# Windowed attention, low-rank mixing and a two-layer MLP in one kernel: the second MLP product's sums built up in one PSUM half, one form of V fewer, a new written-out order

## The chip, the cores and the metric

One Trainium2 chip, one of its cores. A kernel here is a program for five engines that run side by side and meet by semaphores: TensorE (PE; its weight loads are shown as PEld), VectorE (DVE), ScalarE (ACT), GpSimd (POOL) and SyncE (SP), plus the DMA engines that move data between device memory and the on-chip memory SBUF. TensorE writes its results into PSUM, 8 banks of 512 fp32 columns for each of 128 partitions; the other engines fetch them from there. The metric is device time of one execution in microseconds (us), lower is better. A run gives the median of several executions; a profiled execution gives the trace that the sections below read.

## The reference

Four sequences of 768 tokens, 8 heads of 64. Attention with a window of 96 keys and 8 global keys and a linear distance bias, then a mixing of tokens through a matrix of rank 32, then an MLP with a residual:

```python
scores = q @ k.T / sqrt(64) - slope[h] * dist          # dist = 96 for global keys outside the window
a = softmax(where(is_global | is_local, scores, -1e9))
x = (a @ v) as (4, 768, 512)
u = x + ((x.transpose(0, 2, 1) @ U) @ V).transpose(0, 2, 1)    # U 768x32, V 32x768
out = u + relu(u @ w_ch1) @ w_ch2                              # 512 -> 2048 -> 512
```

Inputs and output are fp32; the kernel's products take fp16 and collect in fp32.

## The kernel before

The work is cut into small tasks, each a handful of instructions on one engine, with a name, an estimated duration and the tasks that it needs. The names are used all through this document:

- **Loads.** `lk3`, `lq3`, `lv3`: keys, queries and values of pair 3 (a pair is two heads of one batch; pairs 0 to 3 are batch 0, and so on to 15). `w1_0` to `w1_3`, `w2_0` to `w2_3`: quarters of the MLP weights. All are issued by POOL, but k and q of pair 0 (`lk0`, `lq0`) and U and V (`mixl`) by SP. `Ck0`, `Cq0` cast pair 0 to fp16.
- **Attention of a pair p.** `TKp`, `TQp` transpose on PE, `EKp`, `EQp` copy the result out of PSUM. `KOp` makes a second copy of the keys whose first 32 columns of each block are the global keys; it runs on the engine that the string `KO` names for the pair (A, D, P, or S: a DMA on SP's queue). `VCp`, `VGp` do the same for V. `SBp.s` puts the bias into PSUM (batch 0 only), `Sp.s` adds the scores, `EXp.s` takes exp on ACT, `MKp.s` multiplies by a mask (batches 1 to 3), `PVp` is the product with V, `RCp` and `NMp` normalise into `x_sb`, `XCp` casts to fp16. Pair 3 does this in three parts (`PV3.s`, `RC3.s`, `NH3.s`, `UP3.s`).
- **Mixing.** `UPp` transposes x and multiplies by U, `XEp`, `XUp` turn the result, `TEp` copies it out as `tmp`, `HMp` multiplies by V, `E0p` (for the last pair of a batch `E0p`, `E1p`) copies u, transposed, to `uT`.
- **MLP-1 of batch b**: 16 units n of 128 columns; `M1ab.n` (three of the four inner parts; `M1a`, `M1c`, `M1d` one each for the first units of batch 0) and `M1bb.n` (the fourth), then `RLb.n`, the ReLU on ACT.
- **MLP-2 of batch b**: a 2x2 block product with seven block products instead of eight (Strassen's way, in Winograd's form). `PAb.g`, `PBb.g` form the sums of the ReLU's blocks on DVE, `TWag`, `TWbg` those of w2, once. For each of three tiles t of 128 rows, `RSb.t` puts the low-rank rest (V's forms times `tmp`) into PSUM, and `P1b.t` to `P7b.t` add the seven products, 8 matmuls each. The tasks `DIb.t` to `DHb.t` (D and a letter) then add what lies in PSUM into `x_sb`, and `Ob.t`, `Ob.t+3` store a finished row block through SP.

Two PSUM banks hold a tile's sums: `gX` and `gY`, each of two halves of 256 columns. Before, P1 goes to gX half 0, P6 to gX half 1, P7 to gY half 0, P5 to gY half 1; after they have been fetched P2 goes on in gX half 0, P4 in gY half 0, P3 in gY half 1. The partial sum that four output blocks share is kept in SBUF (`u2`, then `u3`): ACT copies P1 there (`DI`), DVE adds P6 (`DA`) and P7 (`DB`), and the blocks get them from there (`DD`, and `DE`, which adds u2 to two blocks at once).

What sets the order: `ORDER` is a list of all task names written out by hand (or by a search). A planner in the kernel walks through it, gives every task the earliest start that its estimates allow, chooses buffers and PSUM banks, and emits the tasks sorted by these starts. So each engine runs its own tasks strictly in one sequence, and an instruction that waits holds up all behind it on its engine. POOL's queue takes copies and DMA issues in one sequence too. Until MLP-1 of batch 0, the kernel fills gaps that the planner sees on PE with products of zeros (`idle`, L1081).

Of the kernel before, what the change touches and what calls it, by code (L numbers as in the profile page):

```python
# [21 lines left out]
wz iota vz relf rel3 bias6 ones3 bias1 bias4 bias0 lk0 Ck0 TK0 bias3 lq0 Cq0 bias5 SB0.2 TQ0 EQ0 lk1 SB0.0 ones1  # L22
ones0 TK1 EK1 KO1 bias7 lq1 TQ1 EK0 KO0 S0.2 S0.0 SB0.1 S0.1 back bias2 lq3 EQ1 ones2 lk3 TK3 EK3 EX0.0 lk2 lv0
EX0.1 lq2 lv1 lv3 lv2 EX0.2 SB1.2 TK2 S1.2 EX1.2 SB1.0 S1.0 lk4 EX1.0 lq4 SB1.1 mixl lk5 EK2 S1.1 EX1.1 VC0 VG0 TQ3
EQ3 KO2 TQ2 EQ2 PV0 RC0 SB2.2 S2.2 VC3 EX2.2 SB2.1 SB2.0 S2.0 S2.1 EX2.0 VC1 VG1 PV1 KO3 EX2.1 NM0 VG3 RC1 NM1 SB3.2
S3.2 SB3.0 S3.0 SB3.1 S3.1 XC1 EX3.2 EX3.0 VC2 VG2 u16 PV2 UP1 EX3.1 w1_0 vs2 TE1 RC2 NM2 PV3.0 TK4 EK4 vs0 HM1
mask1 E01 PV3.1 RC3.1 NH3.1 XC0 UP0 TQ4 XC2 w1_1 RC3.0 TE0 NH3.0 KO4 UP2 EQ4 HM0 E00 PV3.2 TE2 S4.2 EX4.2 HM2 E02
RC3.2 UP3.0 lq5 UP3.1 NH3.2 UP3.2 NM3 TE3 TD0 S4.0 HM3 E13 E03 M1a0.3 lv4 M1c0.3 w1_2 w1_3 EX4.1 M1d0.3 M1b0.3 RL0.3
M1a0.2 mask3 M1c0.2 w2_2 mask0 TK5 EK5 KO5 w2_0 w2_1 MK4.1 M1d0.2 M1b0.2 w2_3 RL0.2 M1a0.0 M1c0.0 EX4.0 M1d0.0 TQ5
EQ5 M1b0.0 RL0.0 M1a0.7 M1b0.7 S5.0 mask2 M1a0.6 EX5.0 RL0.7 M1b0.6 RL0.6 lk6 MK4.0 EX5.1 VC4 VG4 MK4.2 PV4 M1a0.11  # L30
M1b0.11 M1a0.8 vs3 vs1 RC4 NM4 XC4 RL0.11 lv5 M1b0.8 RL0.8 lk7 PA0.1 PB0.1 S5.2 EX5.2 MK5.0 M1a0.13 M1b0.13 MK5.2
RL0.13 M1a0.10 TWa0 M1b0.10 mask6 lq6 RL0.10 UP4 XE4 TWb0 M1a0.9 M1b0.9 RL0.9 M1a0.14 M1b0.14 RL0.14 lv7 M1a0.15
M1b0.15 MK5.1 M1a0.1 M1c0.1 RL0.15 M1d0.1 XU4 TE4 PA0.3 M1b0.1 RL0.1 M1a0.5 M1b0.5 RL0.5 M1a0.4 M1b0.4 RL0.4 TWa1
TWb1 M1a0.12 M1b0.12 PA0.0 RL0.12 TK6 EK6 PA0.2 RS0.1 P10.1 lv6 DI0.1 HM4 E04 PB0.3 RS0.0 P10.0 VC5 VG5 KO6 PV5 RC5
NM5 TK7 lq7 EK7 TQ6 P50.1 P60.1 EQ6 PB0.0 S6.2 PB0.2 mask7 P20.1 DF0.1 P60.0 mask5 EX6.2 S6.0 P70.1 DI0.0 DA0.0
DE0.0 mask4 EX6.1 MK6.2 P70.0 TQ7 KO7 P20.0 lq8 MK6.1 lk8 P50.0 lq9 EX6.0 DF0.0 DA0.1 MK6.0 DC0.0 VC6 DB0.0 DB0.1
DD0.0 EQ7 XC5 S7.0 lv8 EX7.0 RS0.2 P60.2 MK7.0 VG6 EX7.1 MK7.1 S7.2 EX7.2 P50.2 UP5 XE5 lk9 P10.2 XU5 MK7.2 DC0.2
DE0.1 P40.0 lq10 DC0.1 TE5 HM5 PV6 DI0.2 P20.2 E05 TQ10 EQ10 RC6 NM6 lk10 DA0.2 DE0.2 TK8 VC7 EK8 DG0.0 P30.1 VG7
PV7 TQ8 EQ8 RC7 TK9 NM7 P70.2 TK10 EK10 XC7 XC6 UP6 EK9 P30.2 DH0.1 TQ9 lv9 XE6 XU6 TE6 DH0.2 DB0.2 P30.0 EQ9 HM6
E06 lk11 lq14 UP7 XE7 P40.1 XU7 DD0.2 TE7 P40.2 HM7 DH0.0 KO8 VC8 VG8 S8.2 DF0.2 O0.2 E17 DG0.1 E07 EX8.2 DG0.2  # L40
M1a1.6 M1b1.6 RL1.6 KO9 S9.2 EX9.2 M1a1.9 M1b1.9 O0.1 M1a1.8 RL1.9 M1b1.8 S8.0 EX8.0 MK8.0 lq11 RL1.8 M1a1.13
M1b1.13 RL1.13 TK11 EK11 EX8.1 VC9 TQ11 M1a1.5 M1b1.5 KO11 RL1.5 M1a1.12 M1b1.12 KO10 S10.2 RL1.12 EQ11 S11.2 DD0.1
TD1 O0.5 M1a1.3 M1b1.3 M1a1.0 lk13 O0.3 O0.0 O0.4 MK8.1 EX10.2 RL1.3 MK8.2 PV8 lk12 M1b1.0 RC8 EX11.2 NM8 PA1.2
PB1.2 M1a1.4 RL1.0 M1b1.4 RL1.4 S9.0 EX9.0 MK9.0 EX9.1 MK9.1 M1a1.7 M1b1.7 M1a1.1 RL1.7 MK11.2 M1b1.1 lq12 TQ12
RL1.1 XC8 lq13 UP8 EQ12 M1a1.2 M1b1.2 VG9 M1a1.10 RL1.2 MK9.2 PV9 XE8 PA1.0 PB1.0 RC9 XU8 M1b1.10 lv14 RL1.10
# [12 lines left out]
RL2.7 M1a2.6 M1b2.6 HM14 TE12 PA2.2 PB2.2 HM12 RS2.2 RL2.6 E014 P12.2 PA2.1 PB2.1 E012 PB2.3 RS2.1 S13.0 P12.1 VC15
lv13 DI2.2 DI2.1 VC13 P22.2 DF2.2 P52.1 DC2.1 P22.1 P62.1 DA2.1 DF2.1 EX13.0 P62.2 DA2.2 P72.1 MK13.0 DE2.1 DB2.1
EX13.1 RS2.0 S15.0 EX15.0 EX15.1 P52.2 P12.0 DI2.0 MK13.1 DC2.2 VG15 MK15.1 VG13 PV13 RC13 P42.1 MK15.0 DE2.2 NM13  # L60
P62.0 PV15 RC15 DG2.1 NM15 P72.0 XC13 XC15 P52.0 P32.2 UP13 P32.1 DA2.0 DE2.0 DB2.0 P72.2 UP15 P22.0 DC2.0 DD2.0
XE13 DB2.2 XU13 XE15 XU15 DH2.1 DH2.2 O2.2 TE15 P42.0 HM15 E015 DF2.0 TE13 HM13 P42.2 DG2.2 E013 P32.0 DH2.0 DG2.0
O2.0 E115 M1a3.8 M1b3.8 TD3 M1a3.10 O2.1 RL3.8 M1b3.10 M1a3.7 RL3.10 M1b3.7 M1a3.5 RL3.7 M1b3.5 M1a3.15 RL3.5
M1b3.15 M1a3.2 RL3.15 M1b3.2 M1a3.0 RL3.2 M1b3.0 M1a3.3 RL3.0 M1b3.3 DD2.2 M1a3.1 DD2.1 O2.4 M1b3.1 RL3.3 M1a3.6
RL3.1 M1b3.6 M1a3.12 RL3.6 M1b3.12 RL3.12 M1a3.14 M1b3.14 RL3.14 M1a3.11 M1b3.11 PA3.1 M1a3.9 RL3.11 M1b3.9 M1a3.4
RL3.9 M1b3.4 M1a3.13 M1b3.13 RL3.4 RL3.13 RS3.0 O2.3 RS3.1 PB3.1 PA3.3 PB3.3 RS3.2 P13.0 P13.1 P13.2 DI3.2 PA3.0
PA3.2 P63.1 P53.0 PB3.0 P63.0 PB3.2 P73.0 P73.1 DI3.0 DA3.0 DE3.0 DB3.0 DC3.0 DD3.0 P53.1 P63.2 DA3.2 DE3.2 DI3.1
DA3.1 O2.5 P33.0 DB3.1 P23.2 DF3.2 O3.2a P73.2 DB3.2 P43.1 P43.2 DC3.1 DE3.1 DD3.1 DH3.0 P23.0 DF3.0 O3.0 DG3.1 O3.4
P53.2 DC3.2 DD3.2 DG3.2 O3.5 P23.1 DF3.1 P43.0 DG3.0 P33.1 O3.3 P33.2 DH3.1 O3.1 DH3.2 O3.2
""".split()  # L70
CFG = {
    "NU": (4, 5, 6, 7, 8, 9, 10, 11, 12, 13, 14, 15), "back": "KO1", "early": 4, "Z": (), "ZS": "DDDDDDDD", "ZR": "DDDDDDDD", "ZQ": "DDDDDDDD", "TE": "AADDAADADAAAAAAA", "XE": "DDDDDAADAAAAAAAA", "EK": "ADDDDDAAADADAAAD", "EQ": "DADAADAAAAADAAAA", "KO": "ADDDPPASPPSDAADD",
    "HR": "RRFRRFFRRRFRRRRR", "RR": "RRRRRRRRRRRR", "IB": "ADADDDDA", "U16": "D", "VS": "PPDD", "C0": "DD",
    "VO": "DDPPDPPPPPPPSSPP", "XC": "PDPDDAPDPPPPPPAA", "E": "AAAAAAAADDAAAADA",
}


class Task:
    def __init__(self, name, eng, dur, fn, deps=(), lat=0.1, acq=(), rel=(), size=0.0, parts=1, mode=0, bw=(), br=()):
        self.name, self.eng, self.dur, self.fn = name, eng, dur, fn  # L80
        self.deps = [d for d in deps if d is not None]
        self.lat = lat
        self.acq, self.rel, self.size, self.parts, self.mode = acq, rel, size, parts, mode
        self.start = self.end = None

        self.bw, self.br = bw, tuple(br) + tuple(g for g in rel if g.kind == "ps" and eng != PE)
# [11 lines left out]
class Planner:  # L98
# [41 lines left out]
    def run(self, names):  # L140
# [5 lines left out]
        dma_free = {POOL: 4.1, SP: 0.0}  # L146
        for t in (self.names[n] for n in names):
# [16 lines left out]
            for g in t.acq:  # L164
                if g.since is None:
                    g.since = s
            t.start, t.end = s, s + t.dur
            clock[t.eng] = t.end
# [30 lines left out]
def kernel(  # L199
# [52 lines left out]
    vs = sb("vs", [P, 4, HS], FP16)  # L252
# [3 lines left out]
    N_STG, N_V, N_QK, N_EP, N_X16, N_U = 3, 4, 3, 6, 3, 2  # L256
# [18 lines left out]
    td = sb("td", [P, hd], FP16, 2)  # L275
    sA = sb("sA", [P, 3, hj, HS], FP16)
    tB = sb("tB", [P, 3, hj, hd], FP16)
    u2 = sb("u2", [P, hd], FP32, N_U)
    u3 = sb("u3", [P, hd], FP32, N_U)

    assert hj == H and HS == 384
# [189 lines left out]
    def attention(p):  # L471
# [126 lines left out]
        for pt in parts:  # L598
# [9 lines left out]
            for s in pt:  # L608
                SCs[s] = SC
# [521 lines left out]
```

## Time and profile before

| | |
|---|---|
| median of 3 runs | 229.91 us (229.59, 229.91, 231.64) |
| the profiled execution: its own time | 231.71 us |
| the profiled execution: span from first to last instruction | 229.9 us, granted clock 1.00 |
| start of MLP-1 of batch 0 on PE | 29.40 us |
| MLP-2 of batch 3, first to last product | 208.29 to 226.8 us |
| MLP-1: 512 matmuls of 384 columns | L836 |
| MLP-2: 672 matmuls of 256 columns | L1011 |
| low-rank rest in MLP-2: 48 matmuls | L1001 |

The part of the profile that gives busy time counts an engine as busy while an instruction is in it. For PE the ends of matmuls are modelled, and since they overlap, a busy PE can still have small holes; the distance from one matmul's start to the next one's shows them. The trace has each DMA's issue and its landing; "waits" name what ended an engine's idle time.

### The profile page before, as it was taken

Reading aid. Unit: us, or ns where it says so; the run is one execution under the profiler, and the core shown is the slowest. Engines: PE = TensorE matmul, PEld = TensorE weight load, DVE = VectorE, ACT = ScalarE, POOL = GpSimd, SP = SyncE. Lnnn points to the kernel's source line nnn. Section 1 sums busy time; section 2 is a strip of 40 time slices with the busy share of each in tenths; the row PEclk is TensorE's granted clock in tenths of the full one; section 3 lists DMA queues with packets and bytes.
Section 4 is the critical chain, followed back from the end, with each engine's and each line's share of the span. In section 5 each row is a group of like instructions: output and inputs, shape, how many; then the busy total and the mean of one; then the engine's idle time right before and its main releaser. Section 6 shows DMA issues by size and latency. Waiting matters only on the chain.

```text
span 229.9 us, 5824 instructions
## 1 busy us (share of the span) xinstructions
PE 222.9 (97%) x2455; PEld 161.7 (70%) x2455; DVE 151.8 (66%) x314; ACT 137.4 (60%) x202; POOL 97.4 (42%) x129
## 2 busy tenths in 40 slices
PE   7799989999999999999999999999999999999994
PEld 2466846666888976666798876666689965658883
DVE  7478846789899872499566785445968650067583
ACT  3598887867785568885666448867633246562100
POOL 7879889229994997074932160400001000000000
PEclk9999999999999999999999999999999999999999
DMA  7999899999998999949596173510000043000015
GB/s 171 166 166 118 125 159 206 208 181 137 133 121 55 64 75 230 178 29 105 37 76 63 56 128 138 37 37 0 3 0 3 0 159 119 0 3 0 0 55 222
DMA packets 77193, 21.63 MB, mean 94 GB/s; under 512 B 67280, under 2 KB 74192, under 8 KB 77168
## 3 DMA queue, kind: packets, MB, share of 16 engines
q0 software_dynamic: 68320, 13.24, 68.9%
q1 hardware_dynamic: 8848, 8.03, 10.8%
q8 instruction: 19, 0.31, 0.5%
q14 instruction: 6, 0.05, 0.1%
HBM read 27.46 MB, written 6.29 MB: 147 GB/s over the span
## 4 chain that ended last, share of the span: by engine, by line
PE 89%; DMA 6%; POOL 2%; DVE 1%; issue 0%; POOLq 0%; DVEq 0%
PE ps L836 35%; PE ps L1011 32%; DMA stgq<-in_q_dram 6%; PE ps L591 5%; PE ps L504 3%; PE ps L686 3%; PE ps L659 2%; PE ps L685 2%; PE ps L572 2%; PE ps L780 1%; PE ps L1001 1%; DVE x_sb L1024 1%; PE ps L485 1%; PE ps L664 1%; POOL kO L303 0%; POOL x L748 0%
## 5 line engine op out<-in xcount | busy, mean ns | idle before, releaser
L836 PE MATMUL ps<-uT,w 128*128 128x384 f16 x512 | 87.5, 326 | 0.1
L836 PEld LDWEIGHTS <-w 128*128 128x128 f16 x512 | 48.4, 98 | 31.1 <-issue 0.2
L852 ACT ACTIVATE htr<-ps 128x768 f16<-128x768 f32 x64 | 51.7, 811 | 25.1 <-PE ps L836 24.7
L618 ACT ACTIVATE ep<-ps 128x1024 f16<-128x1024 f32 (+1 forms) x48 | 43.9, 951 | 11.3 <-PE ps L591 10.9
L1011 PEld LDWEIGHTS <-htr 128*128 128x128 f16 x384 | 35.7, 98 | 5.8 <-issue 1.4
L748 POOL CAST x<-x_sb 128x768 f16<-128x768 f32 x9 | 8.2, 910 | 63.7 <-DVE x_sb L724 55.6
L1011 PEld LDWEIGHTS <-sA 128*128 128x128 f16 x288 | 27.3, 98 | 3.7 <-issue 0.4
L1011 PE MATMUL ps<-w,sA 128*128 128x256 f16 x192 | 24.6, 273 | 0.0
L1011 PE MATMUL ps<-w,htr 128*128 128x256 f16 x192 | 24.5, 273 | 0.0
L1011 PE MATMUL ps<-tB,htr 128*128 128x256 f16 x192 | 24.0, 273 | 0.0
L1024 DVE TENSOR_TENSOR x_sb<-ps,x_sb 128x256 f32<-128x256 f32 x48 | 19.4, 417 | 4.8 <-PE ps L1011 4.2
L966 DVE TENSOR_TENSOR sA<-htr 128x768 f16<-128x768 f16 x16 | 9.2, 576 | 19.6 <-ACT htr L852 19.4
L382 POOL DMA_DIRECT2D stgk<-in_k_dram x24 | 20.1, 858 | 4.4 <-DMA w<-in_moe_w_ch_dram 2.8
L382 POOL DMA_DIRECT2D stgq<-in_q_dram x24 | 20.0, 852 | 3.5 <-DMA w<-in_moe_w_ch_dram 3.5
L386 POOL DMA_DIRECT2D vt<-in_v_dram x16 | 16.4, 1033 | 5.7 <-issue 3.6
L631 DVE TENSOR_TENSOR ep<-ep,mask 128x1024 f16<-128x1024 f16 x24 | 17.6, 754 | 0.8 <-ACT ep L618 0.6
L303 POOL COPY vo<-vt 128x660 f16<-128x660 f16 (+1 forms) x22 | 17.3, 789 | 0.5
L724 DVE TENSOR_TENSOR x_sb<-ps,rcp 128x768 f32<-128x768 f32 x16 | 15.2, 952 | 0.5
L1024 DVE TENSOR_TENSOR u<-ps,u 128x256 f32<-128x256 f32 x24 | 10.0, 419 | 8.2 <-PE ps L1011 4.6
L591 PE MATMUL ps<-qT,kT 64*128 64x128 f16 x192 | 14.2, 217 | 0.0
L686 PE MATMUL ps<-vt,ep 128*128 128x65 f16 x192 | 13.6, 193 | 0.0
L686 PEld LDWEIGHTS <-ep 128*128 128x128 f16 x192 | 12.5, 97 | 1.0
(97 smaller groups left out, 321.2 us busy)
## 6 DMA issues: line engine op xcount, KB each, us to landing
out_dram<-x_sb SPq DMA_DIRECT2D x23, 256.0 KB, 2.5
w<-in_moe_w_ch_dram POOLq DMA_DIRECT2D x8, 512.0 KB, 11.2
vt<-in_v_dram POOLq DMA_DIRECT2D x16, 192.0 KB, 5.6
stgk<-in_k_dram POOLq DMA_DIRECT2D x24, 96.0 KB, 5.2
stgq<-in_q_dram POOLq DMA_DIRECT2D x24, 96.0 KB, 4.0
stgk<-in_k_dram POOLq DMA_DIRECT2D x3, 192.0 KB, 6.1
stgq<-in_q_dram POOLq DMA_DIRECT2D x3, 192.0 KB, 7.0
sA<-in_k_dram SPq DMA_DIRECT2D x1, 384.0 KB, 3.1
```

Of the source, the lines that this page charges most:

```text
L303: nc.gpsimd.tensor_copy(dst, src)
L382: nc.gpsimd.dma_start(o[:, i], src[b, h0 + i].rearrange("(n p) d -> p n d", p=P))
L386: nc.gpsimd.dma_start(vt[gv.slot][:, :, :, 0:D], v[b, h0:h0 + 2].rearrange("h (n p) d -> p h n d", p=P),)
L591: nc.tensor.matmul(t[:, hi, j * P:(j + 1) * P], lhs, qt[r, i * P:(i + 1) * P], start=not biased, stop=True, skip_group_check=biased,)
L618: nc.scalar.activation(ep[gep.slot][:, :, lo:512], ps[:, gsc.slot:gsc.slot + 2, lo:512], AF.Exp, scale=qk_scale)
L631: nc.vector.tensor_tensor(ev, ev, mv, ALU.mult)
L686: nc.tensor.matmul(o, e[:, hi, (j + 1) * P:(j + 2) * P], vv[:, hi, i, 0:D1], start=(i == 0), stop=True)
L724: nc.vector.tensor_tensor(xo, pvo()[:, :, :, 0:D], rcp[p % 2].unsqueeze(3).broadcast_to((P, 2, NB, D)), ALU.mult)
L836: nc.tensor.matmul(ps[:, g.slot + half, 0:HS], w1[:, dc, jt * P:(jt + 1) * P], ub[:, dc, half * HS:(half + 1) * HS], start=(dc == flat[0]) ...
L852: nc.scalar.activation(htr[:, jt].rearrange("p (h c) -> p h c", h=2), ps[:, g.slot:g.slot + 2, 0:HS], AF.Relu)
L1011: nc.tensor.matmul(o, a[:, j, c0 + cols.start:c0 + cols.stop], bq[:, j], start=False, stop=(j == hj - 1), skip_group_check=True,)
L1024: return lambda: e.tensor_tensor(o(), x(), y(), ALU.add)
```

## The change

1. **MLP-2's sums.** P1, P6, P7 and P4 go one after the other into gX half 0 without being cleared in between, so that the half holds P1, then P1+P6, and so on. After each one DVE adds the half to the block of x that needs that sum: `DA` (x11), `DB` (x12), `DD` (x22), `DG` (x21). P5 goes to gX half 1, and `DC` adds it to two blocks. P2 and P3 go to the two halves of gY, and `DF` adds both at once, 512 columns wide (in the very last tile two tasks, `DF` and `DH`). `DI` on ACT, `DE`, `u2` and `u3` are gone. P6 now needs DA, P7 needs DB, P4 needs DD.
2. **Three forms of V** (`vs`) in the rest instead of four: V1, V2 and V1-V2. The rest still has four matmuls for a tile.
3. **Bias scalings**: four tasks of 1, 1, 2 and 4 heads instead of eight; three of them on ACT. `Ck0`, `Cq0` on ACT instead of DVE.
4. **Where tasks run** (the strings in `CFG`), for example XC0 on DVE instead of POOL, EQ1 and EQ3 on DVE instead of ACT, KO8 on SP instead of POOL, KO7 and KO10 on POOL instead of SP. `HR` has two F (a full instead of a halved `HM`) instead of four.
5. **The planner's estimates**: POOL's first DMA free at 5.6 instead of 4.1, `lv` 1.4 instead of 1.75, shorter DVE copies with an addition when POOL is at work, the latency of pair 0's loads.
6. **`ORDER`** is new throughout.
7. Code for a seven-product MLP-1 and for another way to the global keys is rewritten or added; the settings `"Z": ()` and `"KG": ()` keep both from running, before and after.

The strings of `CFG` that name the engine of a task by pair (A, D, P, S for ACT, DVE, POOL, SP; R or F for a halved or full `HM`):

```
before EK "ADDDDDAAADADAAAD", EQ "DADAADAAAAADAAAA", KO "ADDDPPASPPSDAADD", HR "RRFRRFFRRRFRRRRR"
after  EK "ADDDAADAAAADDADD", EQ "DDADADAAAAADAADD", KO "ADDDPPPPSDPAPAPP", HR "RRRRRFRRRRFRRRRR"
before VO "DDPPDPPPPPPPSSPP", XC "PDPDDAPDPPPPPPAA", IB "ADADDDDA", C0 "DD", VS "PPDD"
after  VO "DPDPDPDDSPSDPPSD", XC "DDPDDAPPPDDPPADP", IB "DAAA", C0 "AA", VS "DPP"
```

The core of the diff:

```diff
-wz iota vz relf rel3 bias6 ones3 bias1 bias4 bias0 lk0 Ck0 TK0 bias3 lq0 Cq0 bias5 SB0.2 TQ0 EQ0 lk1 SB0.0 ones1
...
-E06 lk11 lq14 UP7 XE7 P40.1 XU7 DD0.2 TE7 P40.2 HM7 DH0.0 KO8 VC8 VG8 S8.2 DF0.2 O0.2 E17 DG0.1 E07 EX8.2 DG0.2
...
+vz wz iota ones3 relf bias1 bias0 bias2 bias4 lk0 Ck0 lq0 Cq0 TK0 rel3 SB0.2 TQ0 EQ0 SB0.0 SB0.1 EK0 lk1 TK1 KO0
...
+SB3.2 EX3.1 SB3.0 S3.0 S3.2 VC3 VG3 PV2 UP1 EX3.0 PV3.0 PV3.1 RC2 EX3.2 PV3.2 vs1 NM2 TE1 lq5 HM1 mask1 w1_0 XC2 E01
+TK4 EK4 RC3.1 NH3.1 UP0 RC3.2 NH3.2 RC3.0 NM3 TK5 EK5 TE0 UP2 TQ4 TE2 lv4 EQ4 HM2 HM0 NH3.0 TQ5 E00 KO4 S4.2 EX4.2
+E02 mask0 EQ5 UP3.0 UP3.1 UP3.2 TE3 HM3 E03 w1_1 KO5 lk6 E13 S4.0 EX4.0 EX4.1 M1a0.0 VC4 VG4 M1c0.0 M1d0.0 M1b0.0
+RL0.0 M1a0.2 M1c0.2 M1d0.2 S5.0 M1b0.2 EX5.1 M1a0.3 RL0.2 M1c0.3 M1d0.3 M1b0.3 RL0.3 MK4.2 MK4.1 vs2 MK4.0 PV4
+M1a0.6 w1_2 M1b0.6 RL0.6 RC4 NM4 M1a0.7 M1b0.7 TK6 EK6 RL0.7 M1a0.11 M1b0.11 EX5.0 M1a0.8 mask2 M1b0.8 XC4 UP4 XE4
...
+lk9 TK9 MK7.1 lk10 XU5 TE5 P20.2 MK7.0 O0.3 HM5 EK9 KO9 P30.1 E05 DC0.1 PV7 TK10 RC7 NM7 lk8 TK8 EK10 P70.2 DD0.2
+DD0.1 EK8 O0.0 TQ9 XC6 UP6 EQ9 XE6 DC0.2 P30.2 DF0.2 KO8 lk11 O0.2 lk12 XC7 lv10 UP7 XE7 XU6 TE6 P40.1 DF0.1 DG0.1
+lq11 HM6 XU7 P40.2 E06 TE7 HM7 E17 S8.2 EX8.2 M1a1.6 E07 DG0.2 M1b1.6 RL1.6 M1a1.9 M1b1.9 RL1.9 S8.0 EX8.1 MK8.1
...
-        dma_free = {POOL: 4.1, SP: 0.0}
+        dma_free = {POOL: 5.6, SP: 0.0}
+        shared_port = []
...
+            if t.eng == DVE and t.fast:
+                t.dur += sum(max(0.0, min(b, s + t.dur) - max(a, s)) * c for a, b, c in shared_port[-20:])
...
-    vs = sb("vs", [P, 4, HS], FP16)
+    vs = sb("vs", [P, 3, HS], FP16)
...
-                    (0, half(gX, 0), tb[:, 0:hd], True), (1, half(gY, 0), tb[:, hd:DM], True),
-                    (3, half(gX, 1), td[b % 2], False), (2, half(gY, 1), td[b % 2], False),
+                    (1, half(gX, 0), tb[:, 0:hd], True), (2, half(gY, 0), tb[:, 0:hd], True),
+                    (1, half(gX, 1), td[b % 2], False), (2, half(gY, 1), tb[:, hd:DM], False),
...
-            P6 = prod(6, gX, 1, sA[:, 1], tB[:, 0], pa[0::2] + c_tb, 2)
-            P7 = prod(7, gY, 0, htr[:, 0:hj], tB[:, 1], pa[1::2] + c_ta, 3, c0=HS)
-            P5 = prod(5, gY, 1, sA[:, 0], w2[:, 0:hj, hd:DM], pa[0::2] + c_ta, 4)
...
+            DA = plus("DA", x11, gX, 0, [P1], rel=[gX])
+            P6 = prod(6, gX, 0, sA[:, 1], tB[:, 0], pa[0::2] + c_tb + [DA])
+            DB = plus("DB", x12, gX, 0, [P6], rel=[gX])
+            P7 = prod(7, gX, 0, htr[:, 0:hj], tB[:, 1], pa[1::2] + c_ta + [DB], c0=HS)
+            DD = plus("DD", x22, gX, 0, [P7], rel=[gX])
+            P4 = prod(4, gX, 0, htr[:, hj:NJC], tB[:, 2], rl_hi + c_tb + [DD], c0=HS)
+            DG = plus("DG", x21, gX, 0, [P4], rel=[gX])
+            P2 = prod(2, gY, 0, htr[:, hj:NJC], w2[:, hj:NJC, 0:hd], rl_hi + c_w2[2:4])
+            P5 = prod(5, gX, 1, sA[:, 0], w2[:, 0:hj, hd:DM], pa[0::2] + c_ta)
+            P3 = prod(3, gY, 1, sA[:, 2], w2[:, hj:NJC, hd:DM], pa[1::2] + c_w2[2:4])
...
+                nc.vector.tensor_tensor(xy, xy, half(gX, 1).unsqueeze(1).broadcast_to((P, 2, hd)), ALU.add)
...
+            DC = add(DVE, 0.7, both, [P5], rel=[gX], name=f"DC{b}.{t}")
...
+                DF = plus("DF", xb[:, t], gY, None, [P2, P3], dur=0.7, rel=[gY])
```

## The prediction

> **What bounds the kernel now.** I read the page's parts 1 and 2 first.
>
> ```profile
> PE 222.9 (97%) x2455; PEld 161.7 (70%) x2455; DVE 151.8 (66%) x314; ACT 137.4 (60%) x202; POOL 97.4 (42%) x129
> PE   7799989999999999999999999999999999999994
> DVE  7478846789899872499566785445968650067583
> ```
>
> TensorE looks full, but a busy PE need not be a full PE, so I went on to busy time by stage (columns: window; busy us and count of PE, PEld, DVE, ACT, POOL; clock; DMA share; GB/s).
>
> ```profile
> 0.00:5.63 5.63, 4.31 (x11) 1.35 (x11) 4.38 (x19) 1.79 (x3) 4.28 (x14) 1.00 0.70 171
> 5.63:16.00 10.37, 9.03 (x163) 5.38 (x163) 6.01 (x11) 7.54 (x11) 9.44 (x11) 1.00 1.59 167
> 16.00:29.40 13.40, 13.34 (x236) 9.48 (x236) 11.26 (x25) 11.49 (x16) 11.05 (x16) 1.00 1.44 128
> 29.40:34.60 5.20, 4.09 (x30) 2.42 (x29) 1.91 (x4) 4.52 (x7) 4.57 (x7) 1.00 1.70 155
> 34.60:207.60 173.00, 172.88 (x1844) 126.30 (x1846) 114.50 (x225) 110.05 (x162) 68.02 (x84) 1.00 0.76 86
> 207.60:229.90 22.30, 19.20 (x180) 16.79 (x180) 13.76 (x32) 1.96 (x4) 0.00 (x0) 1.00 0.19 71
> ```
>
> From 34.6 to 207.6 PE lacks 0.12 us of 173, while DVE has 58 us to spare. The waits of PE and the end of the chain say the same:
>
> ```profile
> PE ps L485 <- DMA stgq<-in_q_dram: 1.3, 1, 1.3
> PE ps L1081 <- POOL zero L314: 1.3, 1, 1.3
> PE ps L504 <- DMA stgq<-in_q_dram: 1.1, 1, 1.1
> ```
>
> ```profile
> 207.59 0.76 PE ps L1001 x12
> 208.35 18.46 PE ps L1011 x168
> 226.84 0.42 DVE x_sb L1024
> ```
>
> PE's own list of waits has three lines: the start, the query load of pair 1 at 9.6, the query load of pair 5 at 34.6. The last MLP-2 runs 168 matmuls without a hole (18.46/168 = 0.11 each, 0.875 a product). So what is removed from DVE or ACT after 34.6 is hidden; time comes only out of the start, or goes in by new waits of PE.
>
> **The change part by part.** The built program keeps every real matmul: 512 of MLP-1, 672 of MLP-2, 48 of the low-rank rest, 352 of scores.
>
> *MLP-2's sums.* Before, a tile has on DVE 4 adds into x (0.417), 2 into u (0.419), one x from u (0.53) and one double (0.80): 3.84, and one ACT copy (0.38). After: 4 quarter adds (0.417), one double add that reads PSUM and one 512-wide add from PSUM. Those two have no row; the nearest are the SBUF double (0.69 to 0.80), two quarter adds (0.83) and the 768-wide normalisation (0.95): 0.75 each, so 3.17. DVE loses 12 x 0.67 = 8 us, ACT 4.6. On the path: **0**, hidden by products; nothing else was late there.
>
> *New waits.* P6 now waits for DA, P7 for DB, P4 for DD, each in one half bank; before, P2, P4 and P3 waited once each for DI, DB, DC. A link needs the last matmul's drain (0.27), the add (0.42) and about 0.1, so some 0.8 us of other PE work between two products. In the built order seven links have under 1.5 us: P6 to P7 of tile 0 of batch 0 (0.88), P1 to P6 of its tile 2 (1.13), P7 to P4 of its tile 0 (1.22), three in batch 2 (1.36 to 1.48) and P7 to P4 of the last tile of batch 3 (0.88). The kernel before has one such link: P7 of its last tile starts at 218.78, its add runs 219.85 to 220.28, P4 starts at 220.52 with no gap. So 0 from below; from above half an instruction of DVE (0.95) in front of each, 7 x 0.48 = 3.3. I take **+0.2**, near the row with no gap. Waiting behind a late product is all of PE.
>
> *Rests, bias, switches.* Three forms of V drop one subtraction (0.54 on DVE) after the start: 0. One halved HM after the start instead of a full one: -0.16. Changes of row mode cost 0.10 to 0.26 of PE each; taken over the two orders they come to about +0.25. Together **+0.1**.
>
> *The start.* The casts of k0 and q0 go to ACT, eight scalings become four; the first transposes can go some 0.7 earlier, but pair 1's loads (landed 7.70 and 9.56) hold either order. From there DVE's new list to TE3 is a chain: EQ1 0.96, KO1 0.87, EK3 0.96, KO3 0.70, VC0 and VG0 1.07, EK2 0.96, KO2 0.40, RC0, NM0, XC0 1.95, EQ3 0.96, VC2 and VG2 0.65, RC1, NM1, XC1 1.98, u16 and vs0 1.28, RC2, NM2 1.18, the halves of pair 3 1.83, NM3 0.95, TE2, E02, EQ5, TE3 1.87: 18.6 us. EQ1 can start at 10.17, so TE3 ends at 28.75; HM3 and S4.0 follow (0.8), and MLP-1 starts at 29.6, against 29.40: **+0.2**. Bounds: with the shortest row of every copy (KO 0.40, VG 0.32, XC 0.56) TE3 is 1.6 earlier, but then w1's first part is later. On POOL it stands behind VC3 (which waits for v3, tenth load as before, 19.5), VG3, vs1, lq5 (1.64): issued by 24.4, landed by before's 4.8 at 29.2, at best 28.5. So 28.5 to 31.
>
> At that start the new order has put TK5 and TQ5 (0.34 each) before it, which the old had after: **-0.68**. Pair 5's query then lands by some 26 and is needed at 27: the wait goes (PE free at 33.32, TQ5 at 34.61): **-1.29**. What is late next is w1's third part: behind XC2 0.83, lv4 1.04, KO4 0.85, w1_1 0.78, KO5 1.39, lk6 1.68, vs2 1.19 it is issued at 32.9 and lands at about 37.0 if the queue in front is served at 2.55 a part and 1.3 a pair; M1a0.11 wants it at 37.8. **+0.2**; above, 2.9 late if it takes the 7.8 us of before.
>
> *Pair 8's shifted keys.* KO8 goes from POOL to a DMA on SP. Its rows (pairs 7 and 10):
>
> ```profile
> kO<-kT SPq DMA_DIRECT2D x2, 120.0 KB, 3.9
> kO<-kT SPq DMA_DIRECT2D x2, 40.0 KB, 4.7
> ```
>
> From the end of EK to the second landing they took 4.5 (pair 7) and, beside output stores, 6.4 from issue (pair 10); there PE had 8.6 and 15.4 us of other work between TK and S. Now it has 5.5: P70.2, TQ9, UP6, P30.2, UP7, P40.1, P40.2 and three small ones. EK8 stands behind EK10 on ACT, so its end is 1.5 after TK8; 1.5 + 4.5 to 6.4 against 5.5 is a wait of 0.5 to 2.4 at S8.2, ahead of batch 1's MLP-1. Behind it stand all of PE, and EX8.2 on ACT. I take **+0.9**, minus the 0.17 that PE lost at this place before.
>
> Sum: 0.2 + 0.1 + 0.2 - 0.68 - 1.29 + 0.2 + 0.9 - 0.17 = -0.54. The tail is as before: last product, one add (0.42), two stores on SP. The profiled execution took 231.71 for a span of 229.9, above the median 229.91 of the runs shown (one of which was 231.64); part of its waits may be its own. I take the difference over: 229.9 - 0.5 = **229.4**.
>
> **Two rules of the Trainium skill.** The ten fillers stand 0.427 apart up to 5.1 and the 512-wide matmuls at 6.09 stand 0.226 apart, so the rate doubles between. The new order issues seven fillers, which end at 4.3, and then PE idles for about 0.5. The Trainium skill ("TensorE: Matmul & The Clock Gate", What's actually happening) has the full clock granted only after a busy window of some 3.4 us, whose phase is free. By that rule the pause could cost a window; that is the rival "slow clock" below.
>
> Casts of one shape took 0.56, 0.77 and 1.04 on DVE, the longest (21.11 to 22.15) beside POOL's issue of w1. The Trainium skill ("SBUF — State Buffer", Who interferes with whom) has VectorE's copies in a two-port mode and GpSimd block one another for a whole instruction. It speaks against putting XC0, VC2 and KO on DVE beside POOL's queue: the rival "long copies".
>
> **Rivals.**
> - *Everything fits* (0.22): the start falls to 28.5 (-1.1), KO8 lands as pair 7's did behind a later S8.2 (-0.9), the two small waits are 0 (-0.4): 227.0. For it: 58 us of idle DVE. Against: w1's first part.
> - *Late weights*, slower than before (0.14): POOL's list makes w1's third part land later than 37.8, and M1a0.11, with PE behind it, waits; at before's 7.8 from issue that is 2.9 instead of 0.2: 232.1. It decides at 0.7 us of delay. Against: before, that part stood behind w1_1, lq5 and lv4, issued within 4.2 us.
> - *Long copies* (0.12): five copies of the start's chain 0.35 longer (the rows spread by 0.47 for KO, 0.43 for VG, 0.48 for XC): +1.7, 231.1.
> - *Chain of adds* (0.07): the seven links at 3.3 instead of 0.2: 232.5.
> - *The wait only moves* (0.06), so that the change doesn't do what its order says: another load is late by 1.3 at a transpose: 230.7.
> - *Slow clock* (0.04): at 0.427 a filler the 3 us of first transposes and scores take 3 more, of which loads hide all but about 1: 230.4.
>
> **How the numbers follow.** My forecast has 0.35. A measurement here tells about 1% from no change: 227.6 and 232.2 are the bounds. Faster by over 1%: most of "everything fits": 0.20. Slower by over 1%: half of late weights, most of the chain of adds, and late weights or long copies coming on top of a KO8 wait of 2.4: 0.20. The rest, 0.60, is within. The range 227.0 to 232.4 leaves out about 2 in 10.
>
> **What would show it.** Right: DVE busy near 143, no ACT copy of u; MLP-1 of batch 0 starting at 29 to 30; no wait of PE for stgq but pair 1's; a wait of PE for the kO transfer near 84; the last 168 matmuls in 18.5 to 18.9. Wrong: PE waits for DVE adds all over MLP-2 (the chain), for w (late weights), or a start outside 28.5 to 31.

## The result, and the profile after

Over 20 executions of each kernel on one chip the median went from 229.86 to **232.69 us**: ratio 1.0106, 95% interval 1.0084 to 1.0127. The forecast was 229.4, the range ended at 232.4. The change made the kernel about 1% slower.

The profiled execution of the kernel after took 231.74 us (span 230.0), at the fast end of its own 20 (231.3 to 235.5), and it looks almost like the profiled execution of before (231.71, span 229.9). So the two pages, laid side by side, show no loss at all. That is the riddle of this case. Busy time and two of the 40-slice rows of the page of after:

```profile
PE 222.3 (97%) x2456; PEld 161.2 (70%) x2456; DVE 148.7 (65%) x295; ACT 132.2 (58%) x185; POOL 93.3 (41%) x125
...
PE   7899999999999989999999999999999999999994
...
DVE  4699853779979642399967666428867740064852
```

DVE lost 3.1 us and ACT 5.2. PE's row has an 8 in its fifteenth slice, 80.5 to 86.3 us, where before it had a 9. Busy time by stage, in windows that answer to those of before (window; busy us and count of PE, PEld, DVE, ACT, POOL; granted clock; DMA share; GB/s):

```profile
5.63:16.00 10.37, 9.27 (x168) 5.44 (x166) 8.18 (x16) 8.54 (x12) 9.99 (x14) 1.00 1.74 179
16.00:29.40 13.40, 12.91 (x229) 9.71 (x231) 11.84 (x24) 11.44 (x17) 11.87 (x18) 1.00 1.60 125
29.40:34.60 5.20, 5.20 (x66) 3.25 (x59) 2.82 (x6) 4.71 (x7) 5.19 (x8) 1.00 1.55 179
34.60:207.60 173.00, 171.64 (x1809) 124.47 (x1804) 110.52 (x211) 103.27 (x146) 61.82 (x76) 1.00 0.74 83
207.60:230.00 22.40, 19.29 (x181) 16.86 (x180) 12.72 (x27) 0.81 (x1) 0.00 (x0) 1.00 0.22 83
```

The hole of 1.1 in 29.4 to 34.6 is filled: pair 5's query is there in time. In its place PE lacks 1.36 us from 34.6 to 207.6, where before it lacked 0.12. PE's waits name it (engine, line, what it waited for: us in total, times, longest):

```profile
PE ps L1123 <- POOL zero L319: 1.3, 1, 1.3
PE ps L604 <- DMA kO<-kT: 1.0, 1, 1.0
...
PE ps L881 <- DMA w<-in_moe_w_ch_dram: 0.3, 1, 0.3
```

The second is `S8.2` at 84.1, waiting for the DMA of KO8 (start, us, instruction, idle before and what ended it):

```profile
84.11 0.23 PE L604 MATMUL ps<-qT,kO 64*128 64x128 f16 x2 [0.97 <-DMA kO<-kT]
```

The matmuls ahead of it, those of HM7, began at 82.80, so from one start to the next it is 1.30; in the kernel before, where S8.2 waits for nothing, the two stand 0.17 apart, so the wait is 1.13. The third is M1a0.11 waiting for w1's third part (0.50 by the same measure, at 38.2). Where the text gives a wait with two decimals, it is measured in this way; the page's lists count only PE's idle time and come out a little lower. No wait for a DVE add of MLP-2 is in the list, and the end of the chain is as it was, 168 matmuls in 18.46:

```profile
207.68 0.76 PE ps L1048 x12
208.44 18.46 PE ps L1056 x168
226.93 0.42 DVE x_sb L1068
```

The sums on DVE, in the groups kept apart by form (xcount, busy us, mean ns):

```profile
L1068 DVE TENSOR_TENSOR x_sb<-x_sb,ps 128x256 f32<-128x256 f32 x50 | 20.1, 415 | 12.3 <-PE ps L1056 11.4
...
L1088 DVE TENSOR_TENSOR x_sb<-x_sb,ps 128x512 f32<-128x512 f32 x12 | 8.0, 677 | 0.8 <-PE ps L1056 0.8
L1068 DVE TENSOR_TENSOR x_sb<-x_sb,ps 128x512 f32<-128x512 f32 x11 | 7.5, 686 | 3.3 <-PE ps L1056 3.1
```

A tile costs 4 x 0.415 + 0.677 + 0.686 = 3.02 on DVE. All three changes of MLP-2's sums are in the trace and none is on the path.

### The profile page after: what moved, and what is told of

Same layout as the page of the kernel before. It is cut to its first block, busy times and chain, and to the rows that moved or that the text cites. A ratio compares the mean times of both kernels' runs of the same rounds, so it can differ in the third digit from the quotient of the medians.

```text
span 230.0 us, 5800 instructions
## 1 busy us (share of the span) xinstructions
PE 222.3 (97%) x2456; PEld 161.2 (70%) x2456; DVE 148.7 (65%) x295; ACT 132.2 (58%) x185; POOL 93.3 (41%) x125
## 4 chain that ended last, share of the span: by engine, by line
PE 79%; DMA 10%; POOL 7%; issue 1%; ACT 0%; DVE 0%; POOLq 0%
PE ps L881 34%; PE ps L1056 31%; DMA vt<-in_v_dram 4%; PE ps L604 4%; DMA w<-in_moe_w_ch_dram 3%; PE ps L514 3%; DMA kO<-kT 2%; PE ps L731 2%; PE ps L704 2%; PE ps L730 1%; POOL stgk L392 1%; DMA sA<-in_k_dram 1%; PE ps L1048 1%; PE ps L825 1%; POOL vt L396 1%
## 5 line engine op out<-in xcount | busy, mean ns | idle before, releaser
L881 PEld LDWEIGHTS <-w 128*128 128x128 f16 x512 | 48.4, 98 | 31.3 <-DMA w<-in_moe_w_ch_dram 0.5
L1068 DVE TENSOR_TENSOR x_sb<-x_sb,ps 128x256 f32<-128x256 f32 (+1 forms) x61 | 27.3, 464 | 15.6 <-PE ps L1056 14.6
L793 POOL CAST x<-x_sb 128x768 f16<-128x768 f32 x7 | 5.9, 838 | 50.5 <-PE ps L709 28.9
L1056 PE MATMUL ps<-w,htr 128*128 128x256 f16 x192 | 23.7, 273 | 0.0
L1056 PE MATMUL ps<-w,sA 128*128 128x256 f16 x192 | 23.6, 273 | 0.0
L308 POOL COPY kO<-kT 128x480 f16<-128x480 f16 (+1 forms) x16 | 9.1, 596 | 23.3 <-DVE kT L304 20.5
L302 ACT ACTIVATE uT<-ps 128x768 f16<-128x768 f32 (+1 forms) x14 | 9.9, 718 | 8.2 <-PE ps L825 8.1
L604 PE MATMUL ps<-qT,kO 64*128 64x128 f16 x160 | 12.3, 218 | 1.4 <-DMA kO<-kT 1.0
```

Of the source, the lines that this page charges most:

```text
L302: nc.scalar.activation(dst, src, AF.Copy)
L604: nc.tensor.matmul(t[:, hi, j * P:(j + 1) * P], lhs, qt[r, i * P:(i + 1) * P], start=not biased, stop=True, skip_group_check=biased,)
L881: nc.tensor.matmul(ps[:, g.slot + half, 0:HS], w1[:, dc, jt * P:(jt + 1) * P], ub[:, dc, half * HS:(half + 1) * HS], start=(dc == flat[0]) ...
L1056: nc.tensor.matmul(o, a[:, j, c0 + cols.start:c0 + cols.stop], bq[:, j], start=False, stop=(j == hj - 1), skip_group_check=True,)
L1068: nc.vector.tensor_tensor(o, o, x, ALU.add)
```

## The experiments

The question was where 2.8 us come from when the two pages differ by nothing. Three theories: **A**, the profiled execution of before is not a usual one, and the wait that the prediction removed from it is its own; **B**, the chain of adds in MLP-2 costs what the page hides; **C**, the new start carries the loss. All ratios are against runs of the kernel before on the same chip beside them.

### Both kernels again

No edit. Before:

> The kernel before, unchanged, profiled once more. Theory A (the profile that I predicted from was a slow execution of it: 231.71 against a median of 229.86, and its waits for the loads of q1 and q5 were its own): a span near 228.0, the wait of PE for q5 at 34.6 (1.29) gone or below 0.3, the start of MLP-1 of batch 0 earlier than 29.40 by up to 0.9. Theory B (what costs is in the changed kernel's MLP-2 sums, the kernel before always has these waits): a span near 229.9 or a faster one in which both waits are still there.

After:

> The changed kernel, unchanged, profiled once more. Its profile had 231.74 against a median of 232.69. Theory A: the waits that vary are those for DMA landings, so the wait at S8.2 for the shifted keys of pair 8 is between 1.3 and 2.4 and the one for w1's third part between 0 and 1.5; no wait of PE for a DVE add between products of MLP-2. Theory B: waits between products of MLP-2 (P6, P7, P4 behind their adds) of 0.2 or more in several places, together about 1.

Before: 229.9 (ratio to itself 1.0014, 95% interval 0.9983 to 1.0045; the two figures behind each ratio below are such an interval). After: 232.99 (1.0122, 1.0078 to 1.0166). The second profiled execution of before had again a long span, 230.2, while eight of its eleven others had 227.3 to 228.3. The second profile of after had 231.4. Two of PE's waits in it:

```profile
PE ps L604 <- DMA kO<-kT: 1.4, 1, 1.4
...
PE ps L881 <- DMA w<-in_moe_w_ch_dram: 0.8, 1, 0.8
```

MLP-1 started at 31.12, because w1's first part landed at 31.1 instead of 29.2, and `S8.2` waited 1.60 (1.77 from start to start). Twice a profile of before came out 2 us above its own median; that speaks for A.

### KO8 on DVE

```diff
-"KO": "ADDDPPPPSDPAPAPP"
+"KO": "ADDDPPPPDDPAPAPP"
```

> The changed kernel with the shifted copy of pair 8's keys made by DVE instead of a DMA on SP; all else as it is. Theory A: the wait of 1.30 before S8.2 goes and nothing takes its place, since DVE has no work between 84.1 and 89.0 and is free at 79.8: 1.3 to 2 less than the changed kernel, so 230.7 to 231.4 at a median of 232.7, a ratio to the kernel before of 1.004 to 1.007. Theory B: less than 0.5 changes, since PE then waits in MLP-2 instead.

232.29 (1.011, 1.0083 to 1.0136), 0.7 below the kernel after beside it, with intervals that overlap. In the trace the wait is gone, and from batch 0's MLP-1 to batch 1's it is 54.08 us instead of 54.88, although w1's third part held PE 0.81 here instead of 0.50. So the DMA is a quarter of the loss by the medians, and a tenth by the ratios.

### The new start alone

The kernel before from MLP-1 of batch 0 on (old sums, four forms of V, old order), with the new order, engines and bias scalings up to there.

> The kernel before from MLP-1 of batch 0 on, with the changed kernel's start: its order and engines for all tasks ahead of M1a0.0, its bias scalings and casts of pair 0; MLP-2 with the old sums and four forms of V. Theory A: the start gives nothing in usual executions, in which the old start has no wait for q5, and MLP-1 can't begin earlier than w1's first part lands (29.2): between equal and 1.2 slower than the kernel before, ratio 1.000 to 1.005. Theory C (the new start is what costs the 2.8): ratio 1.008 to 1.012. By my prediction's sum it would be faster by 1.3 to 1.8, ratio 0.992 to 0.994.

232.04 (1.0102, 1.0067 to 1.0138). C, by its number: the start alone makes nearly all of the loss. It is not the new start to the last detail: the planner has its old estimates here and put 64 products of zeros on PE, where the kernel after has 20. Its windows:

```profile
16.00:31.95 15.95, 14.13 (x263) 11.07 (x258) 12.49 (x24) 11.77 (x17) 15.07 (x21) 1.00 1.57 129
31.95:85.39 53.44, 53.34 (x600) 39.89 (x597) 41.56 (x77) 38.32 (x58) 38.46 (x48) 1.00 1.41 132
85.39:227.72 142.33, 142.33 (x1448) 105.31 (x1447) 86.19 (x181) 77.37 (x115) 30.44 (x37) 1.00 0.44 66
```

From batch 1's MLP-1 to the last product it takes 142.33 with the old sums; the kernel after took 142.45 and, in its second profile, 142.34 with the new ones. MLP-2 of batches 1 to 3 lies in there, and for batch 0 neither profile of after has a wait for an add: **B falls**. What is long is the stretch before MLP-1, which began at 31.95. PE waited there for two query loads:

```profile
PE ps L490 <- DMA stgq<-in_q_dram: 1.3, 1, 1.3
PE ps L509 <- DMA stgq<-in_q_dram: 0.5, 1, 0.5
```

The second is TQ5 itself, at 28.9: the new order has put it ahead of MLP-1, so where pair 5's query is late (28.8 here, 25.6 in the kernel after) it delays the start.

### The old start before the new rest

All tasks ahead of MLP-1 in the old order, the new sums and order behind it.

> The kernel after with the start of the kernel before: all tasks before MLP-1 of batch 0 in the old order and on the old engines (eight bias scalings, casts of k0 and q0 on DVE, pair 5's TK5 and TQ5 behind the first units of MLP-1 again), the new sums, three forms of V and the new order from there on, KO8 still a DMA. If the new start carries the whole loss: 229.9 to 230.9 us (the rest of the change costs 0.1 to 1, most of it KO8's wait at S8.2), about 1.0 to 1.2% below the kernel after. If the loss lies behind the start: 232 to 233, like the kernel after. The profiled execution should show MLP-1 starting near 29.4 if this start's first loads land as in the two profiles of the kernel before (lq1 near 9.6), near 28 if they land earlier.

236.37 (1.0219, 1.016 to 1.0278): a miss of both theories, and of no use for either. Where the two orders meet, PV4 came too early and PE was idle for 2.2 (2.40 from start to start), and for 0.4 at S8.2. MLP-1 itself started at 28.76, earlier than in any profile so far, with lq5 landed at 31.5, not 34.5. With the same order of loads, another execution had them 3 us earlier.

### Pair 5's query later, in the kernel before

```diff
-M1d0.0 TQ5 EQ5 M1b0.0 RL0.0 M1a0.7 M1b0.7 S5.0 mask2 M1a0.6 EX5.0 RL0.7 M1b0.6 RL0.6
+M1d0.0 M1b0.0 RL0.0 M1a0.7 M1b0.7 mask2 M1a0.6 TQ5 EQ5 RL0.7 M1b0.6 S5.0 RL0.6 EX5.0
```

> The kernel before with one move: pair 5's query transpose TQ5, its copy EQ5 and the score S5.0 stand about 2 us later in the order, between units of MLP-1. TQ5 waited 1.29 and 1.14 us for its load in the two profiles. If the usual executions have this wait too: 228.6 to 228.8 (-1.1 to -1.3), 0.5% below the kernel before. If the wait belongs to the profiled executions and the usual ones (spans 227.5 to 228.2 against 229.9 and 230.2) have lost it because all loads land about 1.4 earlier there: 229.7 to 229.9, no change; the profiled execution may still gain 1.2 against the two profiles of the kernel before.

232.78 (1.0126, 1.0104 to 1.0148): neither of the two outcomes. The move took no wait away and made new ones. PE's waits:

```profile
PE ps L685 <- POOL vo L303: 1.0, 1, 1.0
PE ps L686 <- ACT ep L618: 0.7, 1, 0.7
...
PE ps L591 <- DVE qT L299: 0.3, 1, 0.3
```

The last two are PV4 at 38.4 and S5.0 at 37.1, which came 2 us later with the query; up to batch 1's MLP-1 it took 55.86 us. lq5 landed at 32.6 here, before PE would have come to TQ5's old place (33.3 in the first profile): in this execution there was no wait to remove. MLP-1 began at 29.47. The first line of the list stands at 22.4, ahead of what was moved: the last copy of values on POOL, which in the third profile of before, below, holds up nothing, and there MLP-1 began at 28.32. That wait is most of the difference. All five executions lie between 232.5 and 233.1, so the late start is hardly the accident of one; what made the copy late is open.

### w1's first part earlier, and E02 on ACT, in the kernel after

```diff
-lq4 EX2.2 vs0 SB3.1 S3.1
...
-vs1 NM2 TE1 lq5 HM1 mask1 w1_0 XC2
+lq4 w1_0 EX2.2 vs0 SB3.1 S3.1
...
+vs1 NM2 TE1 lq5 HM1 mask1 XC2
```

and in the second kernel also

```diff
-"E": "AADAAAAAAAAADAAA"
+"E": "AAAAAAAAAAAADAAA"
```

> The kernel after with w1_0 issued right behind lq4, that is ahead of VC3, VG3, vs1 and lq5 on POOL (about 4 us earlier), TQ5, EQ5, S5.0, EX5.1 moved behind the first units of MLP-1, and no filler products after 20 us. If the landing of w1's first part sets the start of MLP-1 in the usual executions (it waited 1.02 us in the second profile of the kernel after, 0.95 in the run with the new start alone): 231.3 to 231.8. If DVE's chain up to TE3 sets it: 232.4 to 232.9, at most 0.3 below the kernel after, since TE3 stays near 28.5. A third outcome, slower, if lq5 or w1_1 come too late behind w1_0: 233 to 234.

> The same as the kernel with w1_0 early, and E02 (0.96 us) on ACT instead of DVE, so that DVE's chain up to TE3 is shorter by E02 and by EQ5, 1.5 in all. If the chain on DVE sets the start of MLP-1: 0.5 to 1.3 below the kernel with w1_0 early, that is 231.2 to 232.2. If it is the load of w1: the same as that kernel within 0.3. If PE is the bound there by then (26 to 29 us hold transposes, mixing and scores without much slack): within 0.5.

233.2 (1.0137, 1.0095 to 1.0178) and 232.08 (1.0092, 1.0072 to 1.0113). Both kernels also have TQ5, EQ5, S5.0 and EX5.1 behind the first units of MLP-1 and no zeros after 20 us. In the first, w1's first part landed at 25.1, 4 us earlier than in the kernel after, and MLP-1 still began at 29.37. PE's timeline ahead of it (start, us, instruction, idle before and what ended it):

```profile
28.06 0.34 PE L825 MATMUL ps<-vs,tmp 64*128 64x384 f16 x2 [0.45 <-DVE tmp L304]
...
29.04 0.23 PE L604 MATMUL ps<-qT,kO 64*128 64x128 f16 x2 [0.48 <-DVE uT L304]
```

HM3 waits for TE3 and S4.0 for E03, both on DVE. So with the weights early, DVE's chain holds the start at the same place; with the weights late (31.1, second profile of after) they do. The median of the first lies above what was expected of the chain; a new wait of 0.7 for an exp on ACT, at 35.1, adds to it. The second kernel differs from the first in E02 alone: 1.1 less by the medians, inside what was expected of the chain, but the intervals overlap and its profile shows MLP-1 at 30.41, so that gain is not shown in the trace. The new start has two limits close together, and neither alone is the loss.

### The kernel before, a third time

> The kernel before, unchanged, for one more profiled execution. Theory of the two arrivals: the usual executions (spans 227.5 to 228.4) differ from the two profiled ones (229.9, 230.2) in when the loads land, with nothing else changed. If this execution is a usual one, its profile shows MLP-1 starting at 28.5 to 28.9, w1_1 landed by 31.5, lq5 by 33, and no wait at TQ5. If it is a slow one again: MLP-1 at 29.4 to 29.8, lq5 at 34.5, a wait of 1.1 to 1.3 at TQ5. The theory falls if the span is under 228.5 with lq5 still at 34.5.

229.71, span 227.9: this is a usual execution. PE's waits are now the start and two short ones, none at TQ5:

```profile
PE ps L1081 <- POOL zero L314: 1.3, 1, 1.3
PE ps L485 <- DMA stgq<-in_q_dram: 0.5, 1, 0.5
PE ps L836 <- DMA w<-in_moe_w_ch_dram: 0.3, 1, 0.3
```

```profile
16.00:28.32 12.32, 12.25 (x214) 8.68 (x213) 10.08 (x24) 10.41 (x14) 10.79 (x16) 1.00 1.49 135
28.32:34.60 6.28, 6.28 (x58) 4.02 (x58) 3.69 (x9) 5.75 (x9) 5.58 (x9) 1.00 1.68 166
34.60:82.44 47.84, 47.44 (x554) 36.21 (x549) 38.37 (x71) 33.43 (x50) 36.90 (x46) 1.00 1.47 132
82.44:224.78 142.34, 142.33 (x1448) 105.30 (x1447) 86.33 (x181) 77.38 (x115) 30.45 (x37) 1.00 0.44 66
```

MLP-1 starts at 28.32, not 29.40; w1_1 landed at 30.1 and lq5 at 31.3 (33.2 and 34.5 in the first profile). 1.08 + 1.29 less the 0.36 that M1a0.13 waited here gives the 2.0 between the spans. The loads were ahead from the first on: pair 1's query landed at 7.8, not 9.6, so that the wait of 1.3 for it is down to 0.1. The same stretch of the load stream in three executions of one program (last column: GB/s). First profile:

```profile
26.50:28.00 1.50, 1.46 (x24) 0.93 (x24) 1.09 (x4) 1.37 (x3) 1.50 (x4) 1.00 0.63 55
```

Second:

```profile
26.50:28.00 1.50, 1.46 (x28) 0.95 (x26) 0.77 (x4) 1.37 (x2) 1.50 (x4) 1.00 0.80 106
```

Third:

```profile
26.50:28.00 1.50, 1.46 (x28) 1.25 (x27) 1.47 (x3) 1.50 (x3) 1.50 (x3) 1.00 1.09 167
```

In the first two the loads nearly stood still for a microsecond or more, just ahead of w1_1 and lq5. **A holds**, as far as one usual profile can show it; the next run asks the executions without a trace.

### A probe at TQ5, in the kernel before

```diff
 def go():
+    if p == 5 and stg is stgq:
+        for _ in range(5):
+            nc.tensor.matmul(ps[:, g.slot, 0:512], zero16[:, 0:P], zero16, start=True, stop=True)
     for n in range(NB):
```

> The kernel before with five products of zeros, 512 columns wide (about 1.1 us of PE), in PE's sequence right ahead of TQ5, into the bank that TQ5 clears anyway. If the usual executions wait for pair 5's query there as the two profiled ones did (1.29, 1.14), the zeros lie inside the wait: 229.7 to 230.0, no change. If the usual executions have no such wait, every zero product is paid: 230.8 to 231.1 (+1.1).

231.07 against 229.97 (1.0041, 1.0016 to 1.0065): +1.1 by the medians, +0.9 by the ratio. The zeros are paid nearly in full, so the usual executions have no wait there. The profiled one was the slowest of its own (231.91), and had lq5 at 33.9, 0.2 after the first of the zeros; TQ5 follows them without a hole:

```profile
33.72 1.24 PE L505 MATMUL ps<-zero 128*128 128x512 f16 x5
34.80 0.50 PE L507 MATMUL ps<-ident,stgq 128*128 128x128 f16 x6
```

### The old start once more

The join mended: PV4 and S5.0 where the kernel before has them, KO8 on DVE, the new order from unit 13 of MLP-1 on.

> The new MLP-2 sums, three forms of V and the new order from unit 13 of batch 0's MLP-1 on, behind the start and the first units of MLP-1 in the order of the kernel before, and KO8 on DVE. In the first such join PV4 stood too early and waited 2.4; here PV4, S5.0 and the weights' parts stand as in the kernel before. If the loss lies in the new start, in w1's third part and in KO8: 229.5 to 230.5, level with the kernel before. If the sums or the new order behind the start cost something of their own: 231.5 to 233.

236.02 (1.0179, 1.0114 to 1.0243), again far off, so neither join tells how the new sums and order run behind the old start. Its trace shows what an add of the new sums costs where DVE is behind; PE's longest wait, and DVE's timeline at its end:

```profile
PE ps L1051 <- DVE x_sb L1063: 2.7, 1, 2.7
```

```profile
61.15 0.41 DVE L1063 TENSOR_TENSOR x_sb<-x_sb,ps 128x256 f32<-128x256 f32 x1
...
61.74 0.96 DVE L764 TENSOR_TENSOR x_sb<-ps,rcp 128x768 f32<-128x768 f32 x1
```

DVE formed w2's and the ReLU's sums from 56.7 to 61.2 without a break, `DA` came behind them, and P5 of tile 0, which writes the other half of the bank that `DA` was reading, began as that add ended (61.56, 61.62). So an add of the new sums can hold PE, as the rival "chain of adds" has it, though this is none of the seven links: P5 doesn't need the sum of `DA`, and the add was late because of the other work of DVE. Such a wait isn't in the profiles of the kernel after. What followed this wait is told in the last section.

### The kernel after with its two waits taken away

```diff
-"KO": "ADDDPPPPSDPAPAPP"
+"KO": "ADDDPPPPDDPAPAPP"
-vs2 MK4.0 PV4 M1a0.6 w1_2 M1b0.6
+w1_2 vs2 MK4.0 PV4 M1a0.6 M1b0.6
```

> The kernel after with its two own waits behind the start taken away: KO8 on DVE instead of a DMA (it waited 1.30 and 1.77 at S8.2), and w1_2 issued ahead of vs2 on POOL, about 1 us earlier (M1a0.11 waited 0.50). If these two are paid in full: 231.0 to 231.4 (-1.3 to -1.8 from 232.7), with 53.1 to 53.5 us from the first to the second MLP-1 instead of 54.9, and what is left against the kernel before, 1 to 1.5, lies in the start. If another wait takes their place: 232.2 to 232.7.

231.55 (1.0068, 1.0036 to 1.0099), 1.1 below the kernel after by the medians and 0.9 by the ratios, with intervals that overlap. Its windows from the start of MLP-1:

```profile
30.18:83.58 53.40, 53.01 (x590) 39.34 (x591) 39.61 (x78) 35.08 (x51) 37.06 (x45) 1.00 1.47 147
83.58:226.35 142.77, 142.65 (x1452) 105.21 (x1448) 86.20 (x167) 72.30 (x101) 28.93 (x37) 1.00 0.41 60
```

It took 53.40 instead of 54.88 up to batch 1, as expected. What is left against the usual execution of before adds up: MLP-1 1.86 later (30.18 against 28.32; it waited 1.03 for w1's first part, landed 30.1), 0.72 less up to batch 1 (53.40 against 54.12), 0.43 more behind it: 1.57, and the spans differ by 1.6 (229.5, 227.9).

None of these variants is faster than the kernel before, and its usual execution says why: from 16.0 to the last product PE lacks 0.5 us of 209. Behind 16.0 only less work for PE could help it.

## Why the prediction was wrong

The stages of the profiled executions (us; start of MLP-1 read from PE's timeline):

| | before, first | before, third | after | after, second |
|---|---|---|---|---|
| MLP-1 of batch 0 starts | 29.40 | 28.32 | 29.56 | 31.12 |
| from there to MLP-1 of batch 1 | 55.07 | 54.12 | 54.88 | 54.83 |
| from there to the last product's end | 142.33 | 142.34 | 142.45 | 142.34 |
| span | 229.9 | 227.9 | 230.0 | 231.4 |

**The step that failed** is the last of the sum: "I take the difference over". The sum was made on a profiled execution 1.8 above the median, and the prediction noted that "part of its waits may be its own". It then counted -1.29 for one of those waits and 29.40 for the start, and took the result off a median that has neither. In the usual execution TQ5 waits for nothing, which the third profile shows and the probe bears out, so that term is **0, not -1.29**. MLP-1 starts at 28.32, so the new start at 29.6 is **+1.3, not +0.2**. On the profiles alone the sum looks close (-0.5 predicted, 231.71 to 231.74 measured), but that is luck: an execution of before above its median stands beside one of after below its own.

The other terms, one by one:

- *MLP-2's sums, 0*: right (142.33 before, 142.34 to 142.45 after). A tile's 3.17 on DVE measured 3.02, from 45.3 to 35.6 us in all. But DVE fell to 148.7, not "near 143": I counted what left DVE and not the tasks that the new strings put there.
- *New waits of the adds, +0.2*: no such wait in the profiles of after. That an add can hold PE the second join shows, for 2.7 in one place, behind other work of DVE and at none of the seven links.
- *The start at 29.6, bounds 28.5 to 31*: 29.56 and 31.12. The chain on DVE and the landing of w1's first part (predicted 29.2, measured 29.2 and 31.1) were named rightly as the two limits. That 29.56 was met so closely is luck: pair 1's query landed at 8.2, so EQ1 began at 9.38 and not at 10.17, and the chain took 19.3 us up to TE3 instead of 18.6 (KO2 alone 1.21 instead of 0.40). In the usual execution of before TE3 ended at 27.97 and MLP-1 began 0.35 behind it; in the kernel after it is 28.68 and 0.88.
- *TK5 and TQ5 ahead, -0.68*: with its two waits taken away the kernel after needs 53.40 up to batch 1, before 54.12; less the waits left in each (0.55; 0.36 and 0.18) that is 0.73 less, near the forecast (the small terms of the rests and switches are in it).
- *w1's third part, +0.2*: 0.50. The rival "late weights" (2.9) did not come.
- *KO8 through SP, +0.9, bounds 0.5 to 2.4*: 1.13 and 1.60, inside the bounds and mis-sized by 0.2 to 0.7. In the first profile it was issued at 78.8 and landed at 84.0, 5.2 us.
- *The clock*: the seven fillers still stand 0.427 apart and 0.31 us of idle follow them, but from 5.0 on the matmuls of the transposes follow each other at 0.052, as they do in before from 5.7 on. The pause cost nothing.

With the right ground the same terms give 1.3 - 0.68 + 0 + 0.2 + 0.9 - 0.17 + 0.3 (new waits of the adds, rests and switches) = +1.85, or 229.71 + 1.85 = 231.6; the profiled execution of after took 231.74. By the table the difference is 1.24 in the start, 0.76 up to batch 1 and 0.11 behind it, 2.1 in all, as between the spans. The median of after is 1 higher still. The usual executions of after (median span about 230.9) lie between its two profiles, of which the slower starts MLP-1 1.56 later and waits 0.5 longer for KO8. How often the weights are that late in executions without a trace was not measured.

## What to carry to other kernels

Before a wait in a profile is counted as a gain, compare the profiled execution's own time with the median of the runs: if it is 1% above, some of its waits may be its own, and a wait for a load is the first to suspect. Make the sum against a profile that lies at the median, or test the wait: a microsecond of idle products put in front of the waiting instruction can hide in the wait if it is real, and is paid if it isn't (here 0.9 to 1.1 of 1.1). And when an order that keeps its critical engine full is replaced by one with two nearly equal limits in the start, each of them alone looks harmless and mending one brings the other forward.

## What the runs showed of the hardware

**Landings scatter.** In one unchanged program w1_1, issued 5.8, 7.5 and 7.7 us before it landed, came at 30.1, 33.5 and 33.2; in the kernel after, w1's first part took 6.2 and 7.4 us from its issue. The load stream dips to 55 to 106 GB/s for 1.5 us in some executions and not in others (167). Part of it is the issue: POOL issued w1_1 at 24.4 in the third profile, at 26.0 and 25.5 in the other two. What holds up the rest is open: the trace shows DMAs that fetch instructions near there (16 KB, at 26.1 to 27.0), but in executions of both kinds.

**A wait of 2.7 us was followed by half the clock.** In the second join PE's windows around the wait at 61.6 (PEclk is the column ahead of the last two):

```profile
50.00:58.70 8.70, 8.70 (x95) 6.01 (x93) 8.46 (x12) 5.38 (x7) 4.30 (x5) 1.00 1.95 176
58.70:61.60 2.90, 0.21 (x4) 0.13 (x2) 2.83 (x7) 1.22 (x2) 1.72 (x3) 0.97 1.06 67
61.60:65.00 3.40, 3.38 (x16) 2.16 (x15) 2.93 (x6) 1.26 (x2) 3.40 (x4) 0.52 1.07 68
65.00:70.00 5.00, 5.00 (x60) 4.47 (x59) 2.46 (x5) 2.18 (x3) 0.23 (x2) 1.00 1.14 75
```

In 3.4 us PE began 16 matmuls, two products; elsewhere a product takes 0.875, so 3.4 instead of 1.75, and the wait of 2.7 with what followed cost 4.4. The Trainium skill ("TensorE: Matmul & The Clock Gate", Why this matters for your kernels) advises no idle gap of PE above about 3 us; here half the clock followed a gap of 2.7, so this one trace puts the bound a little lower. The wait of 2.2 in the first join left its profiled execution at 1.00, but three of its five executions had a mean clock of 0.991 to 0.993 and took 236.4 to 237.2, where the other two, at 1.00, took 233.1 and 234.0. One half-speed window of 3.4 us in 230 would give 1 - 0.5 x 3.4/230 = 0.993. So near this bound the same wait may cost now one and now nearly two times its length, but no trace shows it: the three left none, and two executions of the kernel with pair 5's query later, at 0.993 and 0.990, took 233.1 and 232.8, hardly more than its others (232.5 to 232.8).
